# Attention in front of two expert layers: exponentials transposed unscaled, value products scaled by VectorE, one pipeline step less, three score banks, gate columns beside the scores

## Chip, cores and metric

The kernel runs on one core of a Trainium2 chip. The metric is device time in microseconds from the first to the last instruction and what lies around them; 2312.23 us is the median of three runs (2311.88 to 2312.57).

## The reference

Three stages follow each other. First chunked attention for 4 batches, 8 heads, 768 tokens and heads of 64: each chunk of 32 tokens sees 8 memory keys, 16 tokens to its left, itself and 8 to its right. Then two layers with 8 experts of 512 -> 1024 -> 512, of which the first sends each token to one expert (or to none, where a score is not positive), and the second weighs all experts with eight rounds of row and column normalisation. Cut to attention, where the change is:

```python
for c in range(nc):                       # chunk = 32 tokens
    l_start = max(0, c_start - 16); r_end = min(S, c_end + 8)
    k_full = np.concatenate([mem_k, k[:, :, l_start:r_end]], axis=2)
    v_full = np.concatenate([mem_v, v[:, :, l_start:r_end]], axis=2)
    scores = scale * np.matmul(q_c, k_full.transpose(0, 1, 3, 2))
    scores = scores - np.max(scores, axis=-1, keepdims=True)
    a = np.exp(scores)
    a = a / (np.sum(a, axis=-1, keepdims=True) + 1e-09)
    out[:, :, c_start:c_end] = np.matmul(a, v_full)
```

## The kernel before, in words

Attention works through 24 tiles of 128 tokens (NT), with all 8 heads of a tile together. The order of instructions on every engine is written out by hand: each engine takes its instructions in program order, and semaphores between engines do the rest. A tile passes through these steps:

- `load`: keys (kb, three buffers), queries (qs, three), values (vw, four) on SP's queue. Memory keys are copied into place by GpSimd, memory values by small transfers, and zero borders are memset.
- `qk` (L262): for each of two halves p (head parities), one score bank of tag "A" (two banks); a mask matmul opens it, then 32 small score matmuls fill both.
- `smax` (L277): VectorE's maximum of each head, then minus that times the scale, for both halves.
- `sexp` (L285): ScalarE's eight exponentials, which also sum their rows.
- `snorm` (L294): reciprocal of the sums on VectorE, then GpSimd multiplies all exponentials by them.
- `a_trans` (L304): eight transposes on TensorE, two copies out of PSUM on VectorE (L311).
- `av` (L313): products with the values into bank "C".
- `x_evac` (L323): ScalarE copies them to x_nat, and SP stores them to x_t in DRAM.
- `x_trans`, `xt_evac` (L328, L334): x is transposed by TensorE and copied by ScalarE.
- `gate1`, `lp_evac`, `fold1` (L351 to L367): gate logits by four 32-column matmuls into bank "E", copied by ScalarE, folded by one more matmul into bank "F" (fbank).

The loop (L510) runs in step t: evacuations of tiles t-3 and older, `snorm(t-1)`, `a_trans(t-2)`, `qk`, `smax`, `sexp` of tile t, `x_trans(t-3)`, `av(t-2)`, `load(t+2)`, `fold(t-5)`, `gate1(t-4)`. After the last tile of a routing group (GROUPS: 4, 4, 4, 4, 8 tiles) the class `Route` adds its work to the coming steps: choice of the expert, counts, ranks, slots, table. In steps 9, 10, 13, 14, 17, 18 (`convs`) a piece of expert weights is split in a high and a low part: ScalarE casts (L206), VectorE subtracts one step later (L208), and then the next piece is fetched. After the loop the last tiles are drained, the last group of eight is routed, rows are gathered by GpSimd (xe), and the experts start.

Of the kernel before, what the change touches and what calls it, by code (L numbers as in the profile page):

```python
# [19 lines left out]
NM = 8  # L20
# [5 lines left out]
WIN = 88  # L26
KEYS = 96
# [22 lines left out]
def kernel(ctx, tc, qT, kT, v, mem_kT, mem_v, wg, m1_w1, m1_w2, m2_w1, m2_w2, out):  # L50
# [32 lines left out]
    kb = [att.tile([128, 4, NM + 152 + NM], F32, name=f"kb{i}") for i in range(3)]  # L83
    vw = [att.tile([KEYS, 2, D], F32, name=f"vw{i}") for i in range(4)]
    memk_sb = att.tile([128, B, 4, NM], F32, name="memk_sb")

    def load(i):
        b, ib = divmod(i, TPB)
        k, vt = kb[i % 3], vw[i % 4]
        lo, hi = max(0, 128 * ib - 16), min(S, 128 * ib + 136)  # L90
        r = NM + lo - (128 * ib - 16)
        if ib == 0:
            nc.gpsimd.memset(k[:, :, NM:NM + 16], 0.0)
            nc.gpsimd.memset(vt[0:32, 0], 0.0)
        if ib == TPB - 1:
            nc.gpsimd.memset(k[:, :, NM + 144:NM + 152], 0.0)
            nc.gpsimd.memset(vt[64:96, 1], 0.0)
        if i == 0:
            nc.sync.dma_start(out=memk_sb, in_=mem_kT)
        nc.sync.dma_start(out=k[:, :, r:r + hi - lo], in_=kT[:, b, :, lo:hi])  # L100
        nc.sync.dma_start(out=qs[i % 3], in_=qT[:, b, ib])
        if ib < 3:
            for c in (0, NM + 152):
                nc.gpsimd.tensor_copy(out=k[:, :, c:c + NM], in_=memk_sb[:, b])
        for j in range(2):
            g = 2 * ib + j
            lo, hi = max(0, 64 * g - 16), min(S, 64 * g + 72)
            m = NM if j == 0 else 0
            r = m + lo - (64 * g - 16)
            nc.sync.dma_start(out=vt[r:r + hi - lo, j], in_=v[b, lo:hi])  # L110
            if ib < 4 or ib == TPB - 1:
                m = 0 if j == 0 else WIN
                nc.sync.dma_start(out=vt[m:m + NM, j], in_=mem_v[b])


    mask_bf = att.tile([128, 3, 4, KEYS], BF16, name="mask_bf")
    chunk_bf = att.tile([128, 128], BF16, name="chunk_bf")
    one = att.tile([128, 1], F32, name="one")

    nc.gpsimd.memset(chunk_bf, 0.0)  # L120
    nc.vector.memset(one, 0.0)
    nc.scalar.activation(out=one, in_=one, func=ACTF.Exp)
    load(0)
    nc.vector.memset(mask_bf, 0.0)
    for r in range(4):
        nc.vector.memset(chunk_bf[32 * r:32 * r + 1, 32 * r:32 * r + 32], 1.0)
    for j in range(2):
        w = NM * (1 - j)
        nc.vector.memset(mask_bf[64 * j:64 * j + 1, :, :, w + 56:w + WIN], NEG)
        nc.vector.memset(mask_bf[64 * j + 32:64 * j + 33, :, :, w:w + 32], NEG)  # L130
    nc.vector.memset(mask_bf[0:1, 1, :, NM:NM + 16], NEG)
    nc.vector.memset(mask_bf[96:97, 2, :, 80:WIN], NEG)
# [152 lines left out]
    def sexp(i):  # L285
        s, nm = sc.pop(i), ex.pop(i)
        a = att.tile([128, 2, 4, KEYS], F32, name="a", tag="a", bufs=2)
        sm = att.tile([128, 2, 4], F32, name="sm", tag="sm", bufs=2)
        for p in range(2):
            for hp in range(4):  # L290
                nc.scalar.activation(out=a[:, p, hp], in_=s[p][:, hp], func=ACTF.Exp, bias=nm[:, p, hp:hp + 1], scale=scale, accum_out=sm[:, p, hp:hp + 1])  # L291
        ex[i] = a, sm

    def snorm(i):  # L294
        a, sm = ex.pop(i)
        rs = att.tile([128, 2, 4], F32, name="rs", tag="rs", bufs=2)
        nc.vector.tensor_scalar(out=rs, in0=sm, scalar1=1e-9, scalar2=None, op0=ALU.add)
        nc.vector.reciprocal(out=rs, in_=rs)
        t = att.tile([128, 2, 4, KEYS], F32, name="an", tag="an", bufs=2)
        for p in range(2):  # L300
            nc.gpsimd.tensor_tensor(out=t[:, p], in0=a[:, p], in1=rs[:, p].unsqueeze(2).to_broadcast([128, 4, KEYS]), op=ALU.mult)
        an[i] = t

    def a_trans(i, both=False):  # L304
        t = an.pop(i)
        at[i] = att.tile([KEYS, 2, 4, 128], F32, name="at", tag="at", bufs=2)
# [6 lines left out]
    def av(i, tag="C", bufs=1):  # L313
        p = bank("x_ps", tag, bufs)
        t = at.pop(i)
        for hp in range(4):
            for pp in range(2):
# [5 lines left out]
    def x_evac(i):  # L323
# [4 lines left out]
    def x_trans(i, tag="D", bufs=1):  # L328
        p = bank("xt_ps", tag, bufs)
# [10 lines left out]
    lp = {}  # L340
# [9 lines left out]

    def gate1(i, tag="E", bufs=1):  # L351
        p = bank("lp_ps", tag, bufs)
        t = xT.pop(i)
        for k in range(KD):
            nc.tensor.matmul(p[32 * k:32 * k + 32, 0:128], wg_sb[:, k], t[:, k], start=True, stop=True, tile_position=(0, 32 * k))
        lp[i] = p

    def lp_evac(i):
        s = att.tile([128, 128], F32, name="lp", tag="lp", bufs=2)
        nc.scalar.copy(out=s, in_=lp[i][:, 0:128])  # L360
        lp[i] = s
# [13 lines left out]
    class Route:  # L375
# [116 lines left out]
    convs = [9, 10, 13, 14, 17, 18]  # L492
# [6 lines left out]
    def fold(i, t=None):  # L499
        fold1(i)  # L500
        gi, j = where[i]
        if j == GROUPS[gi] - 1:
# [3 lines left out]
            for d, slot, f in ((1, "act", r.logits), (1, "dve", r.choose), (1, "pool", lambda: r.shift(nc.gpsimd)), (2, "act", r.exp), (2, "dve", r.count), (3, "pe", r.rank),  # L506
                               (3, "dve", r.gate), (3, "pool", lambda: r.parts(nc.gpsimd)), (4, "dve", r.slots), (5, "pe", r.table), (6, "dve", r.take)):
                steps.setdefault((t + d, slot), []).append(f)

    for t in range(NT):  # L510
        if t >= 3:
            x_evac(t - 3)
        if t >= 5:
            lp_evac(t - 5)
        if t >= 4:
            xt_evac(t - 4)
        step(t, "act")
        if t >= 1:
            snorm(t - 1)
        if t >= 2:  # L520
            a_trans(t - 2)
        qk(t)
        smax(t)
        sexp(t)
        if t >= 3:
            x_trans(t - 3)
# [11 lines left out]
        if t >= 5:
            fold(t - 5, t)
        if t >= 4:  # L540
            gate1(t - 4)
# [7 lines left out]
    def drain(t):
        for slot in ("act", "dve", "pool", "pe"):  # L550
            step(t, slot)

    x_evac(L - 2)
    xt_evac(L - 3)
    step(NT, "act")
    snorm(L)
    lp_evac(L - 4)
    a_trans(L - 1, True)
    x_trans(L - 2)
    fold(L - 4)  # L560
    gate1(L - 3)
    a_trans(L, True)
    av(L - 1)
    av(L, "A", 2)
    xt_evac(L - 2)
    lp_evac(L - 3)
    x_evac(L - 1)
    fold(L - 3)
    gate1(L - 2)
    x_trans(L - 1)  # L570
    x_evac(L)
# [985 lines left out]
```

## Time and profile before

| what | value |
|---|---|
| median of three runs | 2312.23 us |
| the profiled execution, its span | 2311.72 us, 2309.9 us |
| busy over the span: TensorE, weight loads, VectorE, ScalarE, GpSimd | 99%, 96%, 62%, 53%, 18% |
| first matmul of the experts | 153.3 us |
| granted clock of TensorE, mean | 0.998 |

Times in the rows are microseconds from the first instruction. PE is TensorE, PEld its weight loads, DVE VectorE, ACT ScalarE, POOL GpSimd, SP the queue that issues transfers. A busy TensorE is not TensorE at its peak, because matmuls are pipelined; so durations in the loop are best taken from one start to the next.

### The profile page before, as it was taken

How to read it: one execution, taken by the hardware profiler on the slowest of the kernel's cores; microseconds unless marked ns; L12 is line 12 of the kernel's file. 1: busy time of each engine (PE TensorE's matmuls, PEld its weight loads, DVE VectorE, ACT ScalarE, POOL GpSimd, SP SyncE). 2: the span in 40 equal slices, each digit the busy share in tenths (PEclk: the TensorE clock that was granted, in tenths of full speed). 3: DMA queues.
4: the chain of work that ended last, by engine and by line, in shares of the span. 5: the costliest groups of instructions: out<-in, count | busy, mean ns of one | idle time of the engine just before them, and what ended most of it. 6: DMA issues, size and time to landing. Idle time of an engine off the chain costs nothing.

```text
span 2309.9 us, 49506 instructions
## 1 busy us (share of the span) xinstructions
PE 2276.8 (99%) x20016; PEld 2226.5 (96%) x20016; DVE 1437.4 (62%) x2491; ACT 1217.9 (53%) x2533; POOL 423.3 (18%) x481
## 2 busy tenths in 40 slices
PE   7899999999999999999999999999999999999999
PEld 5788998999999999999999999999999999999999
DVE  5856666677765567556755575558555855576555
ACT  6855545555544455445544564446454644465444
POOL 3433433120001102111111111110211021102001
PEclk9999999999999999999999999999999999999999
DMA  8957757764766757867777687868787777867252
GB/s 245 282 161 246 276 202 269 237 206 152 252 215 181 224 190 219 224 183 220 220 220 195 176 271 192 218 164 265 185 224 190 222 217 203 220 190 209 83 140 80
DMA packets 189587, 477.58 MB, mean 207 GB/s; under 512 B 25192, under 2 KB 54504, under 8 KB 189354
## 3 DMA queue, kind: packets, MB, share of 16 engines
q1 hardware_dynamic: 145706, 380.99, 47.0%
q0 software_dynamic: 43232, 92.72, 21.8%
q8 instruction: 159, 2.61, 0.4%
q14 instruction: 74, 0.61, 0.1%
q10 hardware_dynamic: 416, 0.66, 0.1%
HBM read 342.69 MB, written 118.65 MB: 200 GB/s over the span
## 4 chain that ended last, share of the span: by engine, by line
PE 88%; DVE 3%; ACT 3%; issue 2%; DMA 2%; POOL 1%; POOLq 0%; SPq 0%; ACTq 0%; DVEq 0%
PE h_ps L1004 14%; PE h_ps L1003 14%; PE h_ps L1005 14%; PE y_ps L1081 14%; PE y_ps L1082 14%; PE y_ps L1083 14%; ACT a L291 2%; DVE at L311 1%; PE y_ps L791 1%; PE y_ps L789 1%; DVE mx L281 1%; PE y_ps L790 1%; DMA wraw<-in_m_w_dram 1%; DMA x_t<-x2e,rid 1%; PE h_ps L772 1%
## 5 line engine op out<-in xcount | busy, mean ns | idle before, releaser
L1004 PE MATMUL h_ps<-xs,wh 128*128 128x256 f32 x2688 | 760.1, 283 | 0.1
L1003 PE MATMUL h_ps<-xs,wh 128*128 128x256 f32 x2688 | 757.6, 282 | 0.1
L1005 PE MATMUL h_ps<-xs,wl 128*128 128x256 f32 x2688 | 756.6, 281 | 0.0
L1081 PE MATMUL y_ps<-wh,cb 128*128 128x256 f32 x2304 | 649.3, 282 | 0.0
L1082 PE MATMUL y_ps<-wl,cb 128*128 128x256 f32 x2304 | 647.1, 281 | 0.0
L1083 PE MATMUL y_ps<-wh,cb 128*128 128x256 f32 x2304 | 645.7, 280 | 0.0
L1005 PEld LDWEIGHTS h_ps<-xs,wl 128*128 128x128 f32 x2688 | 507.6, 189 | 0.0
L1003 PEld LDWEIGHTS h_ps<-xs,wh 128*128 128x128 f32 x2688 | 506.6, 188 | 0.5 <-DVE r L896 0.3
L1004 PEld LDWEIGHTS h_ps<-xs,wh 128*128 128x128 f32 x2688 | 504.7, 188 | 0.5 <-DVE xs L915 0.5
L969 DVE TENSOR_TENSOR cb<-r,cb 128x512 fp32r<-128x512 f32 x384 | 265.1, 691 | 324.7 <-ACT cb L979 324.5
L1081 PEld LDWEIGHTS y_ps<-wh,cb 128*128 128x128 f32 x2304 | 435.2, 189 | 0.3
L1083 PEld LDWEIGHTS y_ps<-wh,cb 128*128 128x128 f32 x2304 | 435.2, 189 | 0.0
L1082 PEld LDWEIGHTS y_ps<-wl,cb 128*128 128x128 f32 x2304 | 433.7, 188 | 0.0
L979 ACT CAST cb<-r 128x512 fp32r<-128x512 f32 x384 | 239.4, 624 | 74.5 <-DVE r L971 74.4
L1013 ACT COPY h_ps<-h_ps 128x512 f32<-128x512 f32 x96 | 54.7, 570 | 324.1 <-PE h_ps L1005 324.1
L896 DVE TENSOR_TENSOR r<-h_ps,m 128x512 f32<-128x512 f32 x96 | 66.4, 691 | 200.2 <-PE h_ps L1005 195.3
L970 ACT ACTIVATE cb<-r 128x512 fp32r<-128x512 f32 x96 | 60.6, 631 | 239.7 <-DVE r L896 239.7
L970 ACT ACTIVATE r<-h_ps 128x512 f32<-128x512 f32 x191 | 114.0, 597 | 116.4 <-PE h_ps L1005 113.0
L1121 POOL DMA_DIRECT2D out_dram<-oA x35 | 42.3, 1209 | 636.8 <-ACT wh L206 211.6
L210 DVE TENSOR_TENSOR wl<-wraw,wh 128x512 fp32r<-128x512 f32 (+2 forms) x148 | 125.2, 865 | 48.9 <-ACT wh L206 47.7
L206 ACT CAST wh<-wraw 128x1024 fp32r<-128x1024 f32 (+2 forms) x156 | 114.0, 754 | 47.7 <-DMA wraw<-in_m_w_dram 25.2
L969 DVE TENSOR_TENSOR r<-r,r 128x512 f32<-128x512 f32 x192 | 131.9, 687 | 3.3
(245 smaller groups left out, 3567.5 us busy)
## 6 DMA issues: line engine op xcount, KB each, us to landing
xs<-xd SPq DMA_DIRECT2D x294, 512.0 KB
wraw<-in_m_w_dram SPq DMA_DIRECT2D x124, 512.0 KB
wtt<-in_m_w_dram SPq DMA_DIRECT2D x112, 256.0 KB
xd<-xs SPq DMA_DIRECT2D x42, 512.0 KB
wtt<-in_m_w_dram POOLq DMA_DIRECT2D x56, 384.0 KB, 5.9
td<-wtt SPq DMA_DIRECT2D x42, 512.0 KB
wtt<-td SPq DMA_DIRECT2D x42, 512.0 KB
out_dram<-oA POOLq DMA_DIRECT2D x41, 512.0 KB, 8.9
```

Of the source, the lines that this page charges most:

```text
L206: nc.scalar.copy(out=hi, in_=src)
L210: eng.tensor_tensor(out=lo, in0=src, in1=hi.bitcast(F32), op=ALU.subtract)
L896: add = lambda o, a, b: nc.vector.tensor_tensor(out=o, in0=a, in1=b, op=ALU.add)
L969: tt = lambda o, a, b, op: nc.vector.tensor_tensor(out=o, in0=a, in1=b, op=op)
L970: relu = lambda o, i: nc.scalar.activation(out=o, in_=i, func=ACTF.Relu)
L979: (relu if pos else lambda o, i: nc.scalar.copy(out=o, in_=i))(cb[n, i][:, 0], src)
L1003: nc.tensor.matmul(o, wh[:, SLOT[i], k], x[:, 0, k], start=(new and f == 0 and k == 0), stop=False, skip_group_check=True)
L1004: nc.tensor.matmul(o, wh[:, SLOT[i], k], x[:, 1, k], start=False, stop=False, skip_group_check=True)
L1005: nc.tensor.matmul(o, wl[:, SLOT[i], k], x[:, 0, k], start=False, stop=(k == 1), skip_group_check=True)
L1081: nc.tensor.matmul(o, t[:, 0, c], wh, start=(i != 1 and half == f == j == 0), stop=False, skip_group_check=True)
L1082: nc.tensor.matmul(o, t[:, 0, c], wl, start=False, stop=False, skip_group_check=True)
L1083: nc.tensor.matmul(o, t[:, 1, c], wh, start=False, stop=(half == f == 1), skip_group_check=True)
```

## The change

Weights stay unscaled until after the value products: `a_trans` transposes the raw exponentials, `snorm` only forms the reciprocals (now laid out by head), and `x_norm` multiplies the value products by them on VectorE on the way out of PSUM; GpSimd's multiplication and ScalarE's copy go. `a_trans` and `av` so run in the step after the exponentials, one step earlier than before, and `x_trans`, `gate1` and `fold` move up in the same way. Maximum, exponentials and transposes are issued by halves, with the transposes of the tile before between them. The gate matmuls write columns 384 to 511 of the first score bank of a later tile (bank "E" goes, tag "A" has three banks). Keys and values lie in DRAM in windows with memory rows and borders in place, so that a tile has one load each of keys, queries and values; the first queries are issued by ScalarE. Masks are three tiles, filled one after the other. Weight pieces are converted in five steps instead of six, with the subtraction in two halves; three pieces instead of two are finished at the hand-over to the experts.

```diff
+    def load(i, q=nc.sync):
         b, ib = divmod(i, TPB)
+        q.dma_start(out=qs[i % 3], in_=qT[:, b, ib])
+        nc.sync.dma_start(out=kb[i % 3], in_=kT[:, b, ib])
+        nc.sync.dma_start(out=vw[i % 4], in_=v[b, ib])
...
+    def gate1(i, p=None):
+        p = bank("lp_ps", "A", 3) if p is None else p
+        t = xT.pop(i)
+        for k in range(KD):
+            nc.tensor.matmul(p[32 * k:32 * k + 32, 384:512], wg_sb[:, k], t[:, k], start=True, stop=True, tile_position=(0, 32 * k), skip_group_check=True)
+        lp[i] = p
...
-            s = bank("s_ps", "A", 2)[:, 0:4 * KEYS].rearrange("p (h k) -> p h k", k=KEYS)
-            nc.tensor.matmul(s, chunk_bf, mask_bf[:, mv], start=True, stop=False, skip_group_check=True)
+            s = bank("s_ps", "A", 3)
+            if p == 0 and i >= 3:
+                gate1(i - 3, s)
+            s = s[:, 0:4 * KEYS].rearrange("p (h k) -> p h k", k=KEYS)
+            nc.tensor.matmul(s, chunk_bf, masks[mv], start=True, stop=False, skip_group_check=True)
...
-        for p in range(2):
-            nc.gpsimd.tensor_tensor(out=t[:, p], in0=a[:, p], in1=rs[:, p].unsqueeze(2).to_broadcast([128, 4, KEYS]), op=ALU.mult)
...
+    def x_norm(i):
         x_nat[i] = att.tile([128, D], F32, name="x_nat", tag="x_nat", bufs=3)
-        nc.scalar.copy(out=x_nat[i][:, 0:D], in_=xps.pop(i))
-        nc.sync.dma_start(out=x_t[128 * i:128 * i + 128, :], in_=x_nat[i][:, 0:D])
+        r = ex.pop(i).rearrange("p h q -> p (h q)").unsqueeze(2).to_broadcast([128, H, HD])
+        nc.vector.tensor_tensor(out=x_nat[i].rearrange("p (h d) -> p h d", h=H), in0=xps.pop(i).rearrange("p (h d) -> p h d", h=H), in1=r, op=ALU.mult)
+        nc.sync.dma_start(out=x_t[128 * i:128 * i + 128, :], in_=x_nat[i])
...
-    convs = [9, 10, 13, 14, 17, 18]
+    convs = [4, 7, 11, 15, 19]
...
     for t in range(NT):
+        qk(t)
+        smax(t, 0)
         if t >= 3:
+            lp_evac(t - 3)
+        sexp(t, 0)
+        if t >= 1:
+            a_trans(t - 1, 0, vcopy)
+            a_trans(t - 1, 1, vcopy)
+        smax(t, 1)
+        if t >= 2:
+            x_trans(t - 2)
+            xt_evac(t - 2)
+        sexp(t, 1)
+        if t >= 3:
+            fold(t - 3, t)
+        step(t, "pe")
         if t >= 1:
             snorm(t - 1)
+            av(t - 1)
+            x_norm(t - 1)
+        step(t, "act")
         step(t, "dve")
+        step(t, "pool")
         while defer:
             defer.pop(0)()
+        if t in (1, 2, 3):
             fetch()
         if t + 2 < NT:
             load(t + 2)
```

## Rows read from the trace of the kernel before

**Rows 1.** Windows: busy us (instructions) by engine, clock, DMA share, GB/s.
```profile
43.70:127.30 83.60, 75.45 (x1449) 59.19 (x1448) 63.86 (x201) 67.87 (x318) 38.16 (x77) 1.00 0.86 267
153.30:2309.90 2156.60, 2147.73 (x17706) 2124.21 (x17706) 1338.34 (x2168) 1112.75 (x2052) 360.43 (x333) 1.00 0.69 205
```
**Rows 2.** Chain that ended last, attention loop: start, duration, engine, tile, line.
```profile
7.14 0.57 DVE mx L281
...
10.74 0.48 PE s_ps L268
...
12.74 0.57 DVE mx L281
...
16.74 1.15 DVE at L311 x2
...
43.74 0.47 DVE mx L281
...
127.36 0.48 DVE mx L281
```
**Rows 3.** Order of time, TensorE, one tile: start, duration, line, operation.
```profile
101.77 0.66 PE L331 MATMUL xt_ps<-ident,x_nat 128*128 128x128 f32 x4 [0.94 <-ACT xT L336]
...
102.36 1.15 PE L320 MATMUL x_ps<-vw,at 96*64 96x64 f32 x32
...
103.44 0.40 PE L367 MATMUL fbank<-fold_f,lp 128*128 128x17 f32 x2
...
103.76 0.43 PE L355 MATMUL lp_ps<-xT,wg_sb 128*32 128x128 f32 x8
...
104.12 1.08 PE L310 MATMUL at_ps<-ident,an 128*96 128x128 f32 x8
...
105.45 0.89 PE L275 MATMUL s_ps<-kb,qs 64*64 64x96 f32 x32
```
**Rows 4.** Order of time, VectorE; the first row is the page's group.
```profile
L896 DVE TENSOR_TENSOR r<-h_ps,m 128x512 f32<-128x512 f32 x96 | 66.4, 691 | 200.2 <-PE h_ps L1005 195.3
...
97.40 0.18 DVE L398 TENSOR_REDUCE rmx<-lgs 128x4 f32<-128x32 f32 x1
...
98.51 0.19 DVE L405 SCALAR_TENSOR_TENSOR oh_all<-lgs,rva 128x32 bf16<-128x32 f32 x1
...
103.01 1.22 DVE L208 TENSOR_TENSOR wl<-wraw,wh 128x1024 fp32r<-128x1024 f32 x1
...
104.89 0.17 DVE L297 TENSOR_SCALAR rs<-sm 128x8 f32<-128x8 f32 x1 [0.66 <-ACT a L291]
...
105.21 1.23 DVE L311 COPY at<-at_ps 96x512 f32<-96x512 f32 x2
...
106.38 0.56 DVE L281 TENSOR_REDUCE mx<-s_ps 128x4 f32<-128x384 f32 x1
...
107.05 0.55 DVE L281 TENSOR_REDUCE mx<-s_ps 128x4 f32<-128x384 f32 x1
```
**Rows 5.** Order of time, ScalarE, tile 19.
```profile
106.20 0.66 ACT L336 COPY xT<-xt_ps 128x512 f32<-128x512 f32 x1
...
107.26 0.34 ACT L291 ACTIVATE a<-s_ps,nm 128x96 f32<-128x96 f32 x1 [0.40 <-DVE nm L282]
...
109.49 0.37 ACT L291 ACTIVATE a<-s_ps,nm 128x96 f32<-128x96 f32 x1
```
**Rows 6.** DMA queue (packets, MB, share): 131 to 139, 60 to 120; key load's issue.
```profile
q1 hardware_dynamic: 432, 0.79, 26.6%
...
q1 hardware_dynamic: 14405, 16.99, 90.5%
...
107.93 0.42 SPq L100 DMA_DIRECT2D kb<-in_kT_dram  x1
```
**Rows 7.** Order of time, ScalarE, the last logits.
```profile
140.30 0.27 ACT L391 COPY lgs<-fbank 128x136 f32<-128x136 f32 x1 [0.49 <-PE fbank L367]
```
**Rows 8.** Order of time, TensorE, fold beside rank columns.
```profile
113.54 0.40 PE L367 MATMUL fbank<-fold_f,lp 128*128 128x17 f32 x2 [0.28 <-DVE rt L437]
```

More of the change, by code (lines that the diff above doesn't have):

```diff
@@ L26 @@
 WIN = 88
+KWIN = NM + 152 + NM
 KEYS = 96
@@ L49, with kernel @@
 @with_exitstack
-def kernel(ctx, tc, qT, kT, v, mem_kT, mem_v, wg, m1_w1, m1_w2, m2_w1, m2_w2, out):
+def kernel(ctx, tc, qT, kT, v, wg, m1_w1, m1_w2, m2_w1, m2_w2, out):
     nc = tc.nc
@@ L82 @@
     qs = [att.tile([128, 4, 128], F32, name=f"qs{i}") for i in range(3)]
-    kb = [att.tile([128, 4, NM + 152 + NM], F32, name=f"kb{i}") for i in range(3)]
+    kb = [att.tile([128, 4, KWIN], F32, name=f"kb{i}") for i in range(3)]
     vw = [att.tile([KEYS, 2, D], F32, name=f"vw{i}") for i in range(4)]
-    memk_sb = att.tile([128, B, 4, NM], F32, name="memk_sb")
-    def load(i):
+    def load(i, q=nc.sync):
         b, ib = divmod(i, TPB)
[L89 to L116, printed above, removed]
+        q.dma_start(out=qs[i % 3], in_=qT[:, b, ib])
+        nc.sync.dma_start(out=kb[i % 3], in_=kT[:, b, ib])
+        nc.sync.dma_start(out=vw[i % 4], in_=v[b, ib])
+    masks = [att.tile([128, 4, KEYS], BF16, name=f"mask{i}") for i in range(3)]
     chunk_bf = att.tile([128, 128], BF16, name="chunk_bf")
     one = att.tile([128, 1], F32, name="one")
+    load(0, nc.scalar)
     nc.gpsimd.memset(chunk_bf, 0.0)
@@ L122, with fill_mask @@
     nc.scalar.activation(out=one, in_=one, func=ACTF.Exp)
-    load(0)
-    nc.vector.memset(mask_bf, 0.0)
+    def fill_mask(i):
+        m = masks[i]
+        nc.vector.memset(m, 0.0)
+        for j in range(2):
+            w = NM * (1 - j)
+            nc.vector.memset(m[64 * j:64 * j + 1, :, w + 56:w + WIN], NEG)
+            nc.vector.memset(m[64 * j + 32:64 * j + 33, :, w:w + 32], NEG)
+        if i == 1:
+            nc.vector.memset(m[0:1, :, NM:NM + 16], NEG)
+        if i == 2:
+            nc.vector.memset(m[96:97, :, 80:WIN], NEG)
+    fill_mask(1)
     for r in range(4):
         nc.vector.memset(chunk_bf[32 * r:32 * r + 1, 32 * r:32 * r + 32], 1.0)
[L127 to L132, printed above, removed]
+    fill_mask(0)
     ident = const.tile([128, 128], F32, name="ident")
@@ L207, in split @@
         if defer is not None:
-            defer.append(lambda: nc.vector.tensor_tensor(out=lo, in0=src, in1=hi.bitcast(F32), op=ALU.subtract))
+            for n in range(2):
+                cols = slice(512 * n, 512 * n + 512)
+                defer.append(lambda cols=cols: nc.vector.tensor_tensor(out=lo[:, cols], in0=src[:, cols], in1=hi[:, cols].bitcast(F32), op=ALU.subtract))
             return
@@ L254 @@
     sc = {}
-    an = {}
     at = {}
     ex = {}
+    mn = {}
+    lp = {}
     xT = {}
@@ L260, with lp_evac @@
     xps = {}
+    def gate1(i, p=None):
[4 more added lines that the diff above has]
+        lp[i] = p
+    def lp_evac(i):
+        s = att.tile([128, 128], F32, name="lp", tag="lp", bufs=2)
+        nc.scalar.copy(out=s, in_=lp[i][:, 384:512])
+        lp[i] = s
     def qk(i):
@@ L285, in sexp, with smax @@
[L285 to L292, printed above, removed]
+    def smax(i, p):
+        if p == 0:
+            mn[i] = [att.tile([128, 2, 4], F32, name=k, tag=k, bufs=2) for k in ("mx", "nm")]
+        mx, nm = mn[i]
+        nc.vector.tensor_reduce(out=mx[:, p], in_=sc[i][p], axis=AX.X, op=ALU.max)
+        nc.vector.tensor_scalar(out=nm[:, p], in0=mx[:, p], scalar1=-scale, scalar2=None, op0=ALU.mult)
@@ new lines, in sexp, with a_trans @@
+    def sexp(i, p):
+        if p == 0:
+            ex[i] = att.tile([128, 2, 4, KEYS], F32, name="a", tag="a", bufs=2), att.tile([128, 4, 2], F32, name="sm", tag="sm", bufs=2)
+        a, sm = ex[i]
+        for hp in range(4):
+            nc.scalar.activation(out=a[:, p, hp], in_=sc[i][p][:, hp], func=ACTF.Exp, bias=mn[i][1][:, p, hp:hp + 1], scale=scale, accum_out=sm[:, hp, p:p + 1])
+    def a_trans(i, p, eng):
+        if p == 0:
+            at[i] = att.tile([KEYS, 2, 4, 128], F32, name="at", tag="at", bufs=2)
+        q = bank("at_ps", "B", 2)
+        for hp in range(4):
+            nc.tensor.transpose(q[0:KEYS, 128 * hp:128 * hp + 128], ex[i][0][:, p, hp], ident)
+        eng(out=at[i][:, p], in_=q[0:KEYS])
@@ L294, in snorm @@
     def snorm(i):
-        a, sm = ex.pop(i)
-        rs = att.tile([128, 2, 4], F32, name="rs", tag="rs", bufs=2)
+        sm = ex.pop(i)[1]
+        rs = att.tile([128, 4, 2], F32, name="rs", tag="rs", bufs=2)
         nc.vector.tensor_scalar(out=rs, in0=sm, scalar1=1e-9, scalar2=None, op0=ALU.add)
         nc.vector.reciprocal(out=rs, in_=rs)
-        t = att.tile([128, 2, 4, KEYS], F32, name="an", tag="an", bufs=2)
-        for p in range(2):
-            nc.gpsimd.tensor_tensor(out=t[:, p], in0=a[:, p], in1=rs[:, p].unsqueeze(2).to_broadcast([128, 4, KEYS]), op=ALU.mult)
@@ L302, in snorm, with av @@
[L302 to L306, printed above, removed]
+        ex[i] = rs
+    def av(i):
+        p = bank("x_ps", "C", 1)
+        t = at.pop(i)
         for pp in range(2):
-            p = bank("at_ps", "B", 2)
             for hp in range(4):
-                nc.tensor.transpose(p[0:KEYS, 128 * hp:128 * hp + 128], t[:, pp, hp], ident)
-            (nc.scalar.copy if both and pp else nc.vector.tensor_copy)(out=at[i][:, pp], in_=p[0:KEYS])
@@ L313, in av @@
[L313 to L317, printed above, removed]
                 f = slice(128 * hp + 64 * pp, 128 * hp + 64 * pp + 64)
@@ L339 @@
     lg = {}
-    lp = {}
     fbank = bank("fbank", "F", 1)
@@ L349 @@
     starts = [sum(GROUPS[:g]) for g in range(NGR)]
[L351 to L361, printed above, removed]
     def fold1(i):
@@ L432, in over_c, with places, firsts, slots @@
             return dict(out=self.mo[:, :, c[0]:c[1]], in0=self.ohb.unsqueeze(2).to_broadcast(T), in1=m.unsqueeze(3).to_broadcast(T), op=ALU.mult)
-        def slots(self):
-            nc.vector.tensor_tensor(**self.over_c((3, 5)))
+        def places(self):
             t1 = self.tile("rt1", self.T2)
             nc.vector.tensor_tensor(out=t1, in0=self.rk, in1=self.ohb, op=ALU.mult)
+            nc.vector.tensor_reduce(out=r_all[:, self.i0:self.i0 + self.n], in_=t1, axis=AX.X, op=ALU.add)
+        def firsts(self):
+            nc.vector.tensor_tensor(**self.over_c((3, 5)))
+        def slots(self):
             r = r_all[:, self.i0:self.i0 + self.n]
-            nc.vector.tensor_reduce(out=r, in_=t1, axis=AX.X, op=ALU.add)
             self.oh = []
@@ L505, in fold @@
                 return r
-            for d, slot, f in ((1, "act", r.logits), (1, "dve", r.choose), (1, "pool", lambda: r.shift(nc.gpsimd)), (2, "act", r.exp), (2, "dve", r.count), (3, "pe", r.rank),
-                               (3, "dve", r.gate), (3, "pool", lambda: r.parts(nc.gpsimd)), (4, "dve", r.slots), (5, "pe", r.table), (6, "dve", r.take)):
+            for d, slot, f in ((0, "act", r.logits), (1, "dve", r.choose), (1, "pool", lambda: r.shift(nc.gpsimd)), (2, "act", r.exp), (2, "dve", r.count), (3, "pe", r.rank),
+                               (3, "dve", r.gate), (3, "pool", lambda: r.parts(nc.gpsimd)), (3, "dve", r.places), (4, "dve", r.firsts), (4, "dve", r.slots), (5, "pe", r.table), (5, "dve", r.take)):
                 steps.setdefault((t + d, slot), []).append(f)
+    vcopy, scopy = nc.vector.tensor_copy, nc.scalar.copy
     for t in range(NT):
+        qk(t)
+        smax(t, 0)
         if t >= 3:
[L512 to L517, printed above, removed]
+            lp_evac(t - 3)
[11 more added lines that the diff above has]
+        step(t, "pe")
         if t >= 1:
             snorm(t - 1)
[L520 to L526, printed above, removed]
+            av(t - 1)
+            x_norm(t - 1)
+        step(t, "act")
         step(t, "dve")
+        step(t, "pool")
         while defer:
             defer.pop(0)()
-        step(t, "pool")
-        step(t, "pe")
-        if t in (4, 5):
+        if t == 0:
+            fill_mask(2)
+        if t in (1, 2, 3):
             fetch()
-        if t >= 2:
-            av(t - 2)
         if t + 2 < NT:
             load(t + 2)
[L538 to L541, printed above, removed]
         if t in convs:
@@ L545 @@
         defer.pop(0)()
-    fetch()
     L = NT - 1
[L549 to L555, printed above, removed]
-    snorm(L)
[L557 to L571, printed above, removed]
-    drain(NT)
-    xt_evac(L - 1)
-    lp_evac(L - 2)
-    x_trans(L, "A", 2)
-    drain(NT + 1)
-    drain(NT + 2)
-    fold(L - 2)
+    assert not steps
+    gate1(L - 2)
+    lp_evac(L - 2)
+    for p in range(2):
+        a_trans(L, p, (vcopy, scopy)[p])
+    x_trans(L - 1)
+    xt_evac(L - 1)
+    fold(L - 2)
+    snorm(L)
+    av(L)
+    x_norm(L)
     gate1(L - 1)
+    lp_evac(L - 1)
+    x_trans(L)
     xt_evac(L)
-    gate1(L, "B", 2)
-    lp_evac(L - 1)
+    fold(L - 1)
+    gate1(L)
     lp_evac(L)
-    fold(L - 1)
     q = fold(L)
@@ L594 @@
     q.exp()
+    q.firsts()
+    q.places()
     q.slots()
@@ L834 @@
     held.pop(0)()
+    held.pop(0)()
     xe_trans(0, lambda: busy(14, idle))
     busy(6, idle)
-    held.pop(0)()
-    held.pop(0)()
-    held.pop(0)()
+    while held:
+        held.pop(0)()
     xe_load(2)
@@ L1523, in layout @@
     mk = a["mem_k"].reshape(B, 4, 2, NM, HD).transpose(2, 4, 0, 1, 3)
+    k = np.pad(c(k).reshape(128, B, 4, S), ((0, 0), (0, 0), (0, 0), (16, 8)))
+    mk = c(mk).reshape(128, B, 4, NM)
+    kw = c(np.stack([np.concatenate([mk, k[..., 128 * i:128 * i + 152], mk], axis=-1) for i in range(TPB)], axis=2))
+    v = np.pad(c(a["v"].transpose(0, 2, 1, 3)).reshape(B, S, D), ((0, 0), (16, 8), (0, 0)))
+    mv = c(a["mem_v"].transpose(0, 2, 1, 3)).reshape(B, NM, D)
+    win = lambda i: v[:, 64 * i:64 * i + WIN]
+    vw = c(np.stack([np.stack([np.concatenate([mv, win(2 * i)], axis=1), np.concatenate([win(2 * i + 1), mv], axis=1)], axis=2) for i in range(TPB)], axis=1))
     g = np.concatenate([a["moe_w_gate"], a["moe_w_skip"][:, None], a["moe2_w_gate"]], axis=1)
```

19 lines of the change are left out of this document (5 added, 14 removed).

## The prediction

> **What bounds the kernel now.** I read the windows first, then the chain of waits through the first stage, then each engine's order of time over one tile. From 153.3 us on, TensorE is busy for 2147.7 of 2156.6 us [rows 1]; the change touches nothing there, so it can win only ahead of it. In the attention loop TensorE is busy for 75.5 of 83.6 us, but VectorE for only 63.9 and ScalarE for 67.9 [rows 1]: no engine is full. The chain says why [rows 2]: maximum (DVE mx), exponentials (ACT a), then the two copies of the transposed weights (DVE at), then the next tile's maximum. The next maximum stands behind those copies, and these behind the last exponential, so the tile pays 1.15 (copies) + 0.88 (maximum to first exponential, 106.38 to 107.26) + 8 x 0.318 (exponentials, seven steps from 107.26 to 109.49) + 0.32 (normaliser, 104.89 to 105.21) + some 0.25 of hand-overs = 5.14 [rows 4, 5]. Measured: first maximum of tile 7 at 43.74, of tile 23 at 127.36, 83.6 us for 16 tiles, 5.23 each [rows 2].
>
> **The part sums for one tile after the change.** TensorE keeps every matmul; only their order changes. Start to start: four transposes of x 0.59, value products 1.08, fold 0.32, gate 0.36, eight transposes and the two mask matmuls 1.33 (104.12 to 105.45), scores 0.89 [rows 3]. Sum 4.57. This is its floor, and for the rank matmuls and the table, short ones, I put 0.2 and 0.3 in one tile of four each.
>
> VectorE: two maxima 2 x 0.67 (106.38 to 107.05), copies 1.15, normaliser 0.32, as now: 2.81 [rows 4]. It gains the scaling of the value products out of PSUM, which the trace does not show. Nearest: the 128x512 operation of two tensors, one from PSUM, at 691 ns [rows 4]; bounds: 0.55 (the maximum of 384 elements from PSUM) and 1.22 (1024 elements, 128x1024 subtraction). I take the 691, of which the next instruction sees about 0.62, as it does with the copies (1.23 busy for two, the next maximum 1.17 after the first began). So 3.43. On top come routing and weight work X, by tile modulo 4: table row and choice 1.55 (the choice is six instructions, 97.40 to 98.70 [rows 4], 0.22 each; the other small ones are put near that); two of count and the weight subtraction 1.6 (subtraction 1.22 [rows 4], now two halves); five of gate and places 0.95; five of slots 1.05. Mean 1.29, VectorE total 4.7. GpSimd's multiplications go (nothing else waits for GpSimd in the loop), ScalarE loses the x copy of about 0.5.
>
> So TensorE (4.57 + 0.125) and VectorE (4.7) would both allow 4.7. Do they wait for each other? Let q be the end of a tile's scores, w how late VectorE then still is. The exponentials of the first half start at q + w + 0.92, take 1.27, then ScalarE copies x transposed, 0.66 [rows 5], ending at w + 2.85. The gate matmuls of the next tile need this copy and could otherwise start at 0.91 + 0.59 + 0.32 + 1.08 = 2.90: no margin, so w passes on whole. VectorE scales at max(3.0, w + 2.81), ends 0.62 later, does X. Followed through four tiles: tile A (table 0.3 on TensorE, w = 0.10, X = 1.55): next q at 4.87, w = 0.60. Tile B (X = 1.6): next q at 5.17, w = 0.46. Tile C (rank 0.2, X = 0.95): next q at 5.03, w = 0. Tile D (X = 1.05): 4.57, w = 0.10. Sum 19.64, 4.91 a tile.
>
> **Loads.** Now up to seven issues a tile on SP with key rows of 608 bytes; then four (x out, q, k, v), rows of 2 to 4 KB, 1.26 MB. At the end of the loop only x rows of 2 KB move: 0.79 MB in 26.6% of 16 x 8 us, 23 bytes per ns and engine; between 60 and 120 it is 16.99 MB in 90.5% of 16 x 60 us, 19.6 [rows 6]. With weights 1.46 MB a tile at 16 x 23 is 3.9 us, under 4.9: bandwidth is not short. The lead is. The key load of tile t+2 now is issued at 107.93, 2.5 us after tile 19's scores begin at 105.45 [rows 3, 6], 7.9 us ahead of the need two tiles (10.4 us) later. In the change it queues on SP behind the x store, which waits for the scaling (q + 3.7 to 4.1), so is issued at about q + 4.7 and needed at q + 2 x 4.9 - 0.89 = 8.9. It needs 0.5 to start, 0.65 (x) + 0.65 (q) + 0.85 (k) of transfer and some 0.5 to be reported: 7.4 counted from the x issue at 4.2, in time by 1.5. In the tile of a weight fetch (one in four, 512 KB, 1.3 us, itself behind the subtraction) it comes at about 9.3: 0.4 late. I put 0.1 on the mean: 5.0 a tile, 16 tiles 80.0. **Gain 3.6.**
>
> **Start.** Tile 0's maximum starts at 7.14 [rows 2]. Memory keys no longer come apart with a GpSimd copy, q goes out on ScalarE's queue beside k, the first mask is one third as wide: two issues of some 0.42 [rows 6] less ahead of the data, 0.9 earlier, 6.2. Tile 1's second mask waits for four exponentials of tile 0, not for eight and a used bank: 6.2 + 0.86 + 1.27, 8.4; mask to maximum took 2.0 (10.74 to 12.74 [rows 2]): 10.4. Tile 2 then pays, with TensorE still slow there, about twice 0.91 and 1.08, masks and scores: 16.3. Five tiles at 4.6, 0.4 for the subtraction and 0.6 for the three early weight fetches: tile 7 at 40.3 instead of 43.74. **Gain 3.4.** The third score bank is worth something only here; later the two-bank wait is already covered.
>
> **Drain.** From tile 23's maximum to the last logits is 127.36 to 140.30, 12.9 [rows 2, 7]. Afterwards, from q: last exponential 4.3, second transposes 0.46, ScalarE copy 0.62 with x transposes and fold beside it, value products to 6.85, scaling to 7.6, x transposes to 8.3, copy 9.0, gate 9.4, copy 9.75, fold, logits 10.2. **Gain 2.8.** The routing of the fourth group moves into the loop.
>
> **After it: nothing.** One more weight piece is cast and subtracted at the hand-over (5 instead of 6 in the loop): the cast (1.0) falls into ScalarE's idle while rows are gathered, the half subtractions (1.22 in all) behind the first matmuls of the experts. The ninth piece is fetched only there, about 2 us ahead of its cast; were it late, the first relu would slip by as much, up to 1 us.
>
> Sum: 3.4 + 3.6 + 2.8 = 9.8. The profiled execution took 2311.72 us (span 2309.9 and 1.8 around it), 0.5 under the median of 2312.23. 2311.7 - 9.8 + 0.5 = **2302.4**.
>
> **A rule against it.** The fold matmul of a later tile sat waiting for VectorE's read of rank columns in the same bank, other columns [rows 8]: banks are guarded whole. The Trainium skill, "PSUM — Partial Sum Buffer", section "PSUM bank collisions raise a hardware error", says the same of any two engines, reads against reads included, and asks to guard by bank and quadrant. With gate columns beside the scores, ScalarE's copy of them would then wait for the maximum; by the rows it is done by the time the first exponential could start (0.16 against a gap of 0.27), so I count nothing; by the rule at its worst it is a rival.
>
> **Rivals.** (1) *All waits vanish*: 4.70 a tile, gain 8.4 in the loop, 2297.6. For: w is small in two tiles of four. Against: zero margin at the transposed x. Chance 0.23. (2) *VectorE takes over*: the scaling is nearer its upper bound 1.22, VectorE 5.3 a tile, the loop stays at 5.23: 2306.0. Against: the 691 is the same shape. Chance 0.14. (3) *Shared banks*: the gate copy sits in the exponentials' way, 0.25 a tile in 21 tiles, 5.3: 2307.7. Chance 0.12. (4) *Slower, loads too late*: with the engines 90.5% busy [rows 6] a lead of 7.9 us hides much queueing that one of 4.2 would not. If a key load lands L after its issue at q + 4.7, a tile takes no less than (4.7 + L + 0.89) / 2; by the sum above L is 2.7 without a fetch, 4.6 with one. Break-even is a tile of 5.47 (9.8 given back over 21 tiles), L = 5.4: from there it decides. At L = 6.2, 5.9 a tile, 21 x 0.9 = 19 lost: 2321. Against: less packet time and fewer issues. Chance 0.07. My forecast 0.44, with its own range 2299 to 2306.
>
> **Numbers.** The measurement tells 0.2% (4.6 us) from no change, so faster is below 2307.6. Faster: 0.43 + 0.23 + 0.10 + 0.05 = 0.81; slower 0.06 (rival 4); same 0.13. Range: bounds of the loop (4.6 to 5.4) and start give 2295 to 2309; outside lie rival 4 and tails.
>
> **What would show it.** Right: first maxima 4.9 to 5.1 apart with a pattern of four, tile 7 at 40, tile 23 near 120, logits 10 later, all else shifted. Wrong: score matmuls waiting for key loads by more than 0.5 in most tiles (rival 4), the scaling above 0.8 us (2), exponentials released by the gate copy (3), or a stage behind 153 that changes its length.

## The result, and the profile after

The changed kernel takes 2337.76 us (median; 2334.13 to 2341.24), the kernel before 2312.4 in the same comparison: ratio 1.0109, interval 1.0092 to 1.0127. It is 25 us slower where 10 us faster was forecast. The profiled execution took 2338.85 us (span 2336.1, mean granted clock 0.991).

The windows of the kernel after, busy us (instructions) of TensorE, weight loads, VectorE, ScalarE and GpSimd, then clock, DMA share and GB/s: the loop from the end of tile 7's first maximum to the end of tile 23's (as long as from start to start), the experts from 1.2 us behind their first matmul to the end, and one stretch of 20 us.

```profile
51.80:157.70 105.90, 82.98 (x1458) 68.75 (x1456) 73.91 (x227) 59.97 (x299) 6.30 (x28) 0.87 0.67 205
181.20:2336.10 2154.90, 2146.49 (x17704) 2123.41 (x17702) 1335.27 (x2170) 1113.36 (x2052) 360.98 (x332) 1.00 0.70 205
...
60.00:80.00 20.00, 13.89 (x246) 11.34 (x241) 12.71 (x39) 9.46 (x51) 1.33 (x6) 0.83 0.68 196
```

Against [rows 1]: the experts are as before. The loop takes 105.9 us instead of 83.6, no engine is nearer to full, the transfers are less busy (0.67, was 0.86), and the granted clock, 1.00 before, is 0.87. Every engine's busy share has fallen, so something is waited for.

VectorE in the kernel after, first maxima of tiles 7 and 23, answering to [rows 2]; between them the scaling that [rows 4] could only bound:

```profile
51.23 0.56 DVE L285 TENSOR_REDUCE mx<-s_ps 128x4 f32<-128x384 f32 x1 [5.95 <-PE s_ps L279]
...
60.58 0.69 DVE L323 TENSOR_TENSOR x_nat<-x_ps,rs 128x512 f32<-128x512 f32 x1
...
157.11 0.56 DVE L285 TENSOR_REDUCE mx<-s_ps 128x4 f32<-128x384 f32 x1
```

The scaling is the 0.69 forecast. The maximum of tile 7 waited 5.95 us for scores. What the scores waited for stands in TensorE's order of time, tiles 9 and 10, answering to [rows 3]:

```profile
62.23 0.89 PE L279 MATMUL s_ps<-kb,qs 64*64 64x96 f32 x32 [1.02 <-DMA kb<-in_kT_dram]
63.05 1.08 PE L300 MATMUL at_ps<-ident,a 128*96 128x128 f32 x8
...
66.29 0.50 PE L272 MATMUL s_ps<-mask,chunk_bf 128*128 128x384 bf16 x2
71.75 1.56 PE L279 MATMUL s_ps<-kb,qs 64*64 64x96 f32 x32 [4.96 <-DMA kb<-in_kT_dram]
73.23 1.94 PE L300 MATMUL at_ps<-ident,a 128*96 128x128 f32 x8
```

Tile 10's scores wait 4.96 us for its keys. After that wait the same matmuls take 1.56 instead of 0.89 and 1.94 instead of 1.08: TensorE runs at the lower of its two levels (1.2 instead of 2.4 GHz). After tile 9's wait of 1.02 us they don't. The tile buffer's own view of the kernel after tells how often, up to 160 us:

```profile
its engine sat idle before it (us, times) until:
...
  DMA kb<-in_kT_dram: 36.0, 15
  DMA qs<-in_qT_dram: 3.5, 2
who waited for it (us, times):
...
  PE s_ps L279: 31.4, 13
  PEld s_ps L279: 4.7, 2
...
DMA to landing us min/median/max: 3.9/5.8/7.9
```

The view counts 15 waits, 36.0 us, two of which are the weight loads' (PEld) part of a wait that the matmuls have too; the matmuls alone waited 13 times, 31.4 us. Each of the seven longest of these 13 (1.89 to 4.96 us) was followed by score matmuls of which all or most ran at the lower clock; after none of the shorter ones did they. A key load lands 5.8 us (median) after its issue. SP's order of time (SPq is SP's queue) shows why it is issued late, answering to [rows 6]:

```profile
57.32 0.44 SPq L90 DMA_DIRECT2D kb<-in_kT_dram  x1
...
61.30 0.33 SPq L324 DMA_DIRECT2D x_t<-x_nat  x1
62.95 0.33 SPq L188 DMA_DIRECT2D wraw<-in_m_w_dram  x1
63.40 1.71 SPq L89 DMA_DIRECT2D qs<-in_qT_dram  x1
65.15 0.44 SPq L90 DMA_DIRECT2D kb<-in_kT_dram  x1
...
66.88 0.33 SPq L324 DMA_DIRECT2D x_t<-x_nat  x1
67.31 0.37 SPq L89 DMA_DIRECT2D qs<-in_qT_dram  x1
67.74 0.87 SPq L90 DMA_DIRECT2D kb<-in_kT_dram  x1
```

The store of x waits for the scaling, then the weight fetch for the subtraction, and only then come queries and keys. The keys issued at 57.32, 65.15 and 67.74 are those of tiles 9, 10 and 11; the first two are the ones waited for above.

### The profile page after: what moved, and what is told of

Read it like the earlier page. It is cut to its first block, busy times and chain, and to the rows that moved or that the text cites. A ratio compares the mean times of both kernels' runs of the same rounds, so it can differ in the third digit from the quotient of the medians.

```text
span 2336.1 us, 49229 instructions
## 1 busy us (share of the span) xinstructions
PE 2285.4 (98%) x20016; PEld 2237.9 (96%) x20016; DVE 1451.8 (62%) x2534; ACT 1209.0 (52%) x2508; POOL 375.0 (16%) x393
## 4 chain that ended last, share of the span: by engine, by line
PE 89%; issue 1%; DMA 1%; DVE 1%; ACT 0%; POOL 0%; POOLq 0%; SPq 0%; ACTq 0%; DVEq 0%
PE h_ps L976 14%; PE h_ps L975 14%; PE h_ps L977 14%; PE y_ps L1053 13%; PE y_ps L1054 13%; PE y_ps L1055 13%; PE y_ps L761 1%; PE y_ps L763 1%; PE y_ps L762 1%; PE h_ps L744 1%; PE h_ps L745 1%; PE h_ps L743 1%; DMA wtt<-in_m_w_dram 1%; PE x_ps L898 0%; DVE wl L198 0%
```

## The experiments

Theory: the loads leave too late, behind waiting instructions on SP's queue; the scores wait for keys, and those waits take TensorE's clock down. Rival: the loads leave in time, but the new windowed transfers are slow. All ratios are to the kernel before, run on the same chip in the same comparison.

**Loads at the head of the step.** Same buffers, same lead in tiles, but ahead of the store of x and of the fetch.

```diff
     for t in range(NT):
+        if t + 2 < NT:
+            load(t + 2)
         qk(t)
...
-        if t + 2 < NT:
-            load(t + 2)
```

> The changed kernel with load(t+2) as the first thing of step t, ahead of the x store that waits for the scaling of tile t-1 and of the weight fetch that waits for a subtraction: the same bytes in the same transfers, one tile more of lead. Theory A (the loads leave too late, scores wait for keys, and the waits halve TensorE's clock): the waits for keys, 36 us in the changed kernel, nearly go, the clock stays at full, tiles come 4.9 to 5.1 apart, total 2298 to 2305. Theory B (the transfers themselves, wide windows and few long rows, are too slow or too many at once): tiles stay at 6 or more, total 2325 or more.

Measured 2302.02 us, ratio 0.9953 (0.9937 to 0.997). VectorE's first maxima of tiles 7 and 23, and the windows of the loop and of the experts:

```profile
39.73 0.56 DVE L285 TENSOR_REDUCE mx<-s_ps 128x4 f32<-128x384 f32 x1 [0.79 <-PE s_ps L279]
...
120.49 0.55 DVE L285 TENSOR_REDUCE mx<-s_ps 128x4 f32<-128x384 f32 x1
```

```profile
39.70:120.50 80.80, 75.06 (x1454) 59.90 (x1455) 72.48 (x228) 59.12 (x299) 6.40 (x28) 0.98 0.94 281
145.50:2300.30 2154.80, 2145.00 (x17705) 2122.03 (x17704) 1336.26 (x2170) 1113.01 (x2052) 358.83 (x332) 1.00 0.70 206
```

TensorE's waits for keys fall to 1.6 us, from the 36.0 of the same view above. Moving three issue instructions is worth 36 us, and what is left comes to the total that was forecast; its parts follow further below.

**Loads between store and fetch.** `load(t + 2)` right behind `x_norm(t - 1)`: still behind the store of x, but ahead of the fetch, and of the logits store that some steps have.

> The changed kernel with load(t+2) ahead of the routing step's store and of the weight fetch of the same step, but still behind the x store. Theory A: the seven tiles that came 7 to 10 us after their forerunner (3, 5, 7, 10, 14, 18, 22, all but one behind a fetch) lose 2 to 4 us each with their spells of half clock, the others stay at 5.2 to 6.4: 2312 to 2322. Theory B: same as the changed kernel, 2334 to 2340.

Measured 2318.06, ratio 1.0026 (1.0015 to 1.0037), key waits 22.0 us (36.0 in the kernel after). By the ratios, the fetch and the logits store ahead of the loads account for some 19 us of the 36, the store of x for the other 17.

**The store of x on GpSimd's queue.** Here the store no longer stands ahead of the loads; the fetch does.

```diff
-        nc.sync.dma_start(out=x_t[128 * i:128 * i + 128, :], in_=x_nat[i])
+        nc.gpsimd.dma_start(out=x_t[128 * i:128 * i + 128, :], in_=x_nat[i])
```

> The changed kernel with the x store issued by GpSimd, so that SP's queue no longer stands behind the scaling; a weight fetch still stands ahead of the loads of its step. Theory A: loads leave as soon as their buffers are free, most waits go, some stay in the tiles behind a fetch: 2300 to 2315. Theory B: no gain, 2330 or more.

A miss, close to what the expectation had for Theory B (2330 or more): 2329.0, ratio 1.0071 (1.0051 to 1.0092). But SP's own waits in this run say where the wait went:

```profile
SPq L188 <- DVE wl L196: 48.6, 5, 11.2
SPq L377 <- ACT lgs L376: 30.2, 4, 9.6
```

With the store gone, SP runs ahead and stands at the weight fetch (waiting for the subtraction, up to 11.2 us) and at the logits store, with the loads behind them. It is not one instruction that holds the loads up, but any waiting one ahead of them on an in-order queue.

**The kernel before with only the new windowed loads.**

> The kernel before with only the new loads (one transfer each for keys, queries and values, memory rows and borders already in place); order and everything else as before. Theory A: the layout is harmless where the lead is long: 2306 to 2313. Theory B: the wide transfers are what is slow: 2325 or more.

Measured 2311.38, ratio 0.9995 (0.9986 to 1.0005). The layout is harmless; the rival falls.

**The kernel before with its loads late.**

```diff
         if t >= 3:
             x_evac(t - 3)
+        if 1 <= t < NT - 1:
+            load(t + 1)
...
-        if t + 2 < NT:
-            load(t + 2)
```

> The kernel before with nothing changed but the place of its loads: those of tile t+1 are issued in step t behind the store of x, instead of those of tile t+2 at the end of step t. If the late issue is the cause, this kernel too waits for keys (over 0.5 us in most tiles), its clock falls in the loop, and it takes 2320 to 2345. If the changed kernel's own structure is the cause (its shorter depth, its shared banks), this one stays at 2310 to 2318.

Measured 2325.91, ratio 1.0058 (1.0038 to 1.0078). A later issue alone makes the old kernel slower by about 13 us: it now waits for queries and keys, and the clock falls to 0.83 between 40 and 60 us:

```profile
PE s_ps L275 <- DMA qs<-in_qT_dram: 13.6, 12, 1.8
...
PEld s_ps L275 <- DMA kb<-in_kT_dram: 7.2, 3, 2.6
```

**What the halved clock costs: work in the waits.** The changed kernel, with constant transposes into columns that nobody reads, in the seven tiles with the longest waits.

```diff
                 gate1(i - 3, s)
+            if p == 1 and i in (3, 5, 7, 10, 14, 18, 22):
+                busy(32, s[:, 384:512])
```

> The changed kernel with its late loads as they are; in the seven late tiles (3, 5, 7, 10, 14, 18, 22) TensorE gets 32 transposes of a constant, about 4.3 us of work, into unused columns ahead of the second mask, so that it works while the keys are awaited. If the halved clock behind each wait is a good part of the loss, the granted clock stays at 1.00 and the time falls from 2337.8 to 2320 to 2330. If the waiting alone is the loss, and the clock only falls where TensorE would wait anyway, the time stays at 2334 or more although the clock is up.

Measured 2333.89, ratio 1.0086 (1.007 to 1.0103), mean clock 0.998. This lies a tenth of a microsecond below the 2334 of the expectation's second case, in which the waiting alone is the loss. But in three of the seven tiles (5, 7 and 18) the filler ended only about 0.1 us ahead of the scores, as at tile 5 here, so that it may have held them up itself:

```profile
34.77 1.80 PE L77 MATMUL s_ps<-ident 128*128 128x128 f32 x15
36.66 0.89 PE L281 MATMUL s_ps<-kb,qs 64*64 64x96 f32 x32
```

So once more, with 22 transposes:

> The run with filler again, with 22 transposes instead of 32 (about 2.5 us instead of 3.7) in the same seven tiles: in three of them the filler of 32 ended only 0.1 us before the scores, so it may itself have held them up. If that hid a gain from the full clock, the time now falls to 2322 to 2330 with the granted clock still at 0.98 or more in the loop. If the clock is worth little because the tile waits for its keys anyway, 2331 to 2338.

Measured 2324.59, ratio 1.0059 (1.0045 to 1.0072). Its window from 60 to 80 us, beside the one of the kernel after shown above (clock 0.83):

```profile
60.00:80.00 20.00, 18.40 (x347) 15.88 (x342) 15.67 (x49) 12.95 (x66) 1.58 (x7) 1.00 0.84 257
```

At full clock in most of the loop the changed kernel is 1.0109 - 1.0059, about 0.5% or 12 us, faster, with its loads in the same place behind store and fetch. So of the 36 us between it and the run with early loads, at least some 12 are the clock (at least: in tiles 3, 5 and 10 the scores again follow the filler without a wait, so it may still delay them), and up to 24 the waiting.

**Is the transfers' rate short too?** Loads at the head of the step, and 256 KB more a tile.

```diff
         nc.sync.dma_start(out=vw[i % 4], in_=v[b, ib])
+        if i >= 2:
+            nc.sync.dma_start(out=spare[i % 2], in_=qT[:, b, ib])
```

> The changed kernel with loads at the head of the step (2302.0), and one more load of 256 KB a tile, into a buffer that nobody reads. If the transfers' rate is not short, as the forecast had it (3.9 us a tile against 4.9), 0.85 us more a tile fit and the time is 2302 to 2305. If it is short (the queue was busy for 95% of its engines' time at 286 GB/s), a tile takes 1.72 MB / 301 GB/s = 5.7 us and the time is 2311 to 2317.

Measured 2314.54, ratio 1.0015 (1.0005 to 1.0024): 12 to 14 us (by medians or by ratios) for the 22 tiles with an extra load, about 0.6 each. The queue (packets, MB, share of 16 engines) between 20 and 120 us, in this run:

```profile
q1 hardware_dynamic: 15383, 30.69, 101.9%
```

It is full at 307 GB/s. The forecast's "bandwidth is not short" had a margin of 1 us a tile (3.9 against 4.9); of 0.86 us more transfer a tile only about 0.25 was hidden. Part of the 0.6 is again the clock, which is 0.83 in this run between 20 and 40 us; how much was not tried. The Trainium skill, "DMA: Bandwidth & Descriptors", section "Where 436 GB/s comes from", puts the memory's side of such transfers at some 358 GB/s. The mean of this mix of loads and stores, 307, stays below that.

**Two score banks instead of three**, with loads at the head (tag "A" with two banks).

> The changed kernel with loads at the head of the step (2302.0), and two score banks instead of three. By the forecast the third bank is worth something at the start only: the second mask of tile 1 waits for eight exponentials instead of four, some 1 to 1.5 us, so 2302.5 to 2305, tile 7's maximum about 1 later and 16 tiles as before. A rival: the mask of a tile's second half waits in every tile for the last exponential of the tile before, 0.3 us or more a tile, 2308 or more.

Measured 2311.11, ratio 0.9998 (0.9989 to 1.0008): the rival of the expectation. TensorE, one tile and the next:

```profile
64.56 0.32 PE L272 MATMUL s_ps<-mask,chunk_bf 128*128 128x384 bf16 x1 [0.62 <-ACT a L293]
64.81 0.89 PE L279 MATMUL s_ps<-kb,qs 64*64 64x96 f32 x32
...
68.88 0.34 PE L272 MATMUL s_ps<-mask,chunk_bf 128*128 128x384 bf16 x1
69.84 0.32 PE L272 MATMUL s_ps<-mask,chunk_bf 128*128 128x384 bf16 x1 [0.62 <-ACT a L293]
```

In every tile the second mask waits 0.62 us for the last exponential, and tiles come 5.28 apart (64.56 to 69.84). At the start the second mask of tile 1 comes at 10.26 instead of 9.08, the 1 to 1.5 expected; but tile 7's maximum is then 4.9 us late (44.62 for 39.73), not 1. The third bank is worth 9 to 10 us, nearly all of the 10.4 that the run with early loads wins.

**More lead, and less work on VectorE.** Three runs on top of the loads at the head of the step: loads of tile t+3 with one more buffer each; the loop's weight subtractions on GpSimd; both.

> The changed kernel with the loads of tile t+3 (not t+2) at the head of step t, with one more buffer each for queries, keys and values. If what is left of the load waits (1.6 us for keys, 3.8 for queries in the run with loads at the head of the step) still costs, 2297 to 2300. If VectorE (77 of 80 us busy there) or the rate of the transfers holds the tile, another step of lead gives nothing: 2300.5 to 2303.

> The changed kernel with loads at the head of the step t (2302.0), and the weight subtractions of the loop (two of 0.69 us in each of five tiles) on GpSimd instead of VectorE. If VectorE is the loop's bound, as the forecast's four tiles had it (the tile with the subtraction 0.5 longer than it would be), 2297 to 2300. If the transfers hold the tile (1.41 MB at 301 GB/s is 4.7 us on the mean, with up to 5.9 in the tile of a fetch), 2301 to 2303.

> Both of them: loads of tile t+3 at the head of step t with a buffer more, and the loop's weight subtractions on GpSimd. If VectorE was the bound and the leads cover the tiles of a fetch, 2293 to 2298, with tiles of 4.7 to 4.8. If the transfers are the bound, 2299 to 2302.

Measured 2300.93 (0.9949, 0.9935 to 0.9962), 2302.31 (0.9954, 0.994 to 0.9967) and 2299.71 (0.9958, 0.9944 to 0.9972). None can be told from the run with loads at the head (0.9953). With the deeper loads no wait for keys is left among the largest waits, so what was left of them cost nothing that the total shows. (VectorE's "77 of 80 us busy" in the first of these expectations is a misreading: it is 72.48 of 80.8, in the window above.) The subtraction's move gives nothing, and VectorE, GpSimd and ScalarE show why in the tile of a subtraction (second run):

```profile
87.10 0.55 DVE L285 TENSOR_REDUCE mx<-s_ps 128x4 f32<-128x384 f32 x1
87.69 0.78 DVE L286 TENSOR_SCALAR nm<-mx 128x4 f32<-128x4 f32 x1
88.38 1.27 DVE L301 COPY at<-at_ps 96x512 f32<-96x512 f32 x2
```

```profile
87.17 2.50 POOL L196 TENSOR_TENSOR wl<-wraw,wh 128x512 fp32r<-128x512 f32 x2 [0.73 <-ACT wh L192]
```

```profile
88.56 0.34 ACT L293 ACTIVATE a<-s_ps,nm 128x96 f32<-128x96 f32 x1 [0.55 <-DVE nm L286]
```

The scaling of the maximum, four elements a partition, takes 0.78 instead of 0.17: it ends at 88.47, where the first half of GpSimd's subtraction does (87.17 + 1.25 = 88.42). In four of the five tiles with a subtraction it is stretched so (0.60 to 1.11). Here the first exponential waits 0.55 us for it, and the tile takes 5.10 (87.10 to 92.20), where it took 5.15 with the subtraction on VectorE. The Trainium skill, "SBUF — State Buffer", section "Who interferes with whom", says that VectorE's multiply by a constant and GpSimd can shut each other out for a whole instruction; these rows agree.

## Why the prediction was wrong

**The step that failed is "Loads".** It said: key load issued at q + 4.7, landing 2.7 us later, in time by 1.5, and 0.4 late behind a weight fetch, "0.1 on the mean". The issue time without a fetch was right in the tile shown above: tile 9's scores ended at about 63.05, the keys of tile 11 were issued at 67.74, q + 4.7. Three terms were not.

- *The landing*: 5.8 us on the median, 3.9 at the least, not 2.7. Two things were left out. The rate of 23 bytes per ns and engine was read from the end of the loop, where only x rows move; the other row of [rows 6], 19.6, was the loop's own, and the changed kernel's is 19.3 (28.48 MB in 70.8% of 16 x 130 us). At 19.3 the terms of the step give 0.85 (x) + 0.85 (q) + 1.11 (k) + 1.0 = 3.8, counted from the store's issue like the forecast's, so 3.3 from the keys', still under the least measured. And the sum began with an empty queue, where the values of the tile before (0.39 MB, 1.3 us by the same rate) or a weight piece (0.52 MB, 1.7 us) can still stand in it: 4.6 to 5.0, an estimate. The rest to 5.8 is not accounted for. The 1.0 for start and report was read from no row, and no run shows it by itself; the shortest landing in the kernel after's table of transfers is 2.4 us (median, 16 KB of logits), with other bytes in the queue.
- *The fetch*: tile 8's scores ended at about 57.2. The store went out at q + 4.1, as forecast; the fetch only at q + 5.75, behind the subtraction, then the queries' issue itself took 1.71 us (why, the profile doesn't say), and the keys left at q + 7.9. They landed at q + 14.5, where 9.3 was forecast.
- *The clock* had no price at all. The 4.96 us wait shown above was followed by matmuls at 1.2 GHz, and filling the longest waits gave back some 12 us.

Rival 4 had the mechanism, the condition (a landing of 5.4 us or more) and the side, but only 0.07 of the chance, and its price, 2321 at a landing of 6.2, lacked the clock: with the waits filled, at full clock, the kernel took 2324.6.

**The other steps**, read from the run with the loads at the head, where theirs is the only term removed (us; the parts add up to the span, the last row is the median):

| | before | forecast | after | loads at the head |
|---|---|---|---|---|
| tile 7's first maximum | 43.7 | 40.3 | 51.2 | 39.7 |
| 16 tiles | 83.6 | 80.0 | 105.9 | 80.8 |
| to the last logits | 12.9 | 10.2 | 9.6 | 9.8 |
| to the experts' first matmul | 13.0 | 13.0 | 13.3 | 14.3 |
| from there to the end | 2156.6 | 2156.6 | 2156.1 | 2155.7 |
| total | 2312.4 | 2302.4 | 2337.8 | 2302.0 |

The last logits of the kernel after and of the run with loads at the head, answering to [rows 7]:

```profile
166.66 0.27 ACT L376 COPY lgs<-fbank 128x136 f32<-128x136 f32 x1 [0.49 <-PE fbank L352]
```

```profile
130.25 0.27 ACT L376 COPY lgs<-fbank 128x136 f32<-128x136 f32 x1 [0.70 <-PE fbank L352]
```

- *Loop*: the forecast counts a tile from one end of the scores to the next, 4.87, 5.17, 5.03 and 4.57 for tiles A to D (redone from its own terms, B and C come to 5.12 and 4.98). In the run with deeper loads, where no keys are waited for, the transposes right behind the scores start at 61.08, 65.61, 70.59, 75.73 and 80.23: 4.53, 4.98, 5.14 and 4.50, in sum 19.15 against 19.64. Most of the difference lies in A, where the table's matmuls, put at 0.3, cost nothing (4.53 against 4.50 in D). The run with loads at the head has the same 19.15 for its undisturbed tiles (first maxima 4.98, 5.14, 4.50 and 4.53 apart), but some 4 us over its 16 tiles go elsewhere: TensorE idles 1.51 us ("issue") in the value products at 43.03, after which the clock falls and two tiles lose 2.6, and 1.20 us in the same way at 84.51. What it waited for there, the profile doesn't say; it stays open.
- *Start and drain*: right within 0.6 us each, the start partly by luck: tiles 0 and 1 have their maxima 0.6 and 0.7 later than worked out (6.77 and 11.08), tile 2 0.6 earlier (15.67).
- *Third bank*: "worth something only here; later the two-bank wait is already covered" was wrong, though the sum was not touched by it. Without the bank 16 tiles take 84.5 us (tile 7's to tile 23's maximum) instead of 80.8, because the last exponential is waited for in every tile.
- *Hand-over*: counted at nothing, bounded at 1 us for the ninth weight piece; 0.3 longer in the kernel after, 1.3 in the profile of the run with early loads. There it is the clock once more, 0.64 between 130 and 134 us: the 14 constant transposes ahead of the rank matmuls take 2.61 us, as against 1.72 in the kernel before (second line), in the kernel after and with the subtraction moved.

```profile
131.01 2.61 PE L77 MATMUL w_ps<-ident 128*128 128x128 f32 x14
```

```profile
140.65 1.72 PE L76 MATMUL w_ps<-ident 128*128 128x128 f32 x14
```

- *Shared banks* [rows 8]: ScalarE's copy of the gate columns does wait for VectorE's maximum, here in the kernel after; VectorE's row (the constant's product) is the one that the exponential needs:

```profile
63.73 0.17 DVE L286 TENSOR_SCALAR nm<-mx 128x4 f32<-128x4 f32 x1
```

```profile
63.79 0.27 ACT L260 COPY lp<-s_ps 128x128 f32<-128x128 f32 x1 [2.06 <-DVE mx L285]
64.00 0.34 ACT L293 ACTIVATE a<-s_ps,nm 128x96 f32<-128x96 f32 x1
```

The exponential starts at 64.00, 0.1 after the product's end at 63.90: near the nothing that was counted in this tile, and not the 0.25 of rival 3.

So the total of the run with early loads, 2302.0 against 2302.4 forecast, is close by luck too, because errors cancel: the undisturbed tiles are a little shorter than worked out, TensorE's idle stretches and the spell of lower clock at the hand-over were not in the sum.

## What to carry to other kernels

When a change moves a load's issue, follow everything ahead of it on its queue, and take the landing time from rows of the same loop with the queue as full as it is there, not from a quiet stretch. A long wait on TensorE's path can cost more than its length, because what follows it can run at half the clock (some 12 of 36 us here); price it so, or give the engine work to do that ends before the wait does. On an in-order queue put the instructions that wait for nothing ahead of those that wait.

## What the runs showed of the hardware that was not expected

- After key waits of 4.43 us (tile 7) and 4.96 us (tile 10) TensorE's clock was at its lower level, and 32 score matmuls took 1.56 instead of 0.89 us; 2.5 us of constant transposes in each of the seven longest waits raised the mean clock of the run from 0.991 to 0.998 and were worth 12 us net.
- The DMA queue of this loop was full at 307 GB/s (101.9% of its 16 engines' time); at 281 GB/s (94%) a load of 256 KB a tile could no longer be added for nothing.
- A VectorE instruction on four elements a partition took up to 1.11 us instead of 0.17 while GpSimd subtracted 128x512 tiles.
